# Top-32 attention with a routed expert layer: where three small steps of a row tile's end are put

## The chip, the cores and the metric

One Trainium2 chip, one core. The metric is the device time of one execution in microseconds; it is given as the median of several runs. TensorE (PE), VectorE (DVE), ScalarE (ACT), GpSimd (POOL) and SyncE (SP) each work through a queue of their own in order; semaphores hold an instruction back until others have finished.

## The reference

Attention over 8 batches, 8 heads, 576 rows of 64 features: only the 32 largest scores of a row are kept. Its result is the input of an expert layer: a gate with 8 experts, of which each keeps its 80 best tokens.

```python
scores = scale * np.matmul(q, k.transpose(0, 1, 3, 2))
kth = np.partition(scores, -top_k, axis=-1)[..., -top_k:-top_k + 1]
scores = np.where(scores >= kth, scores, -1000000000.0)
scores = scores - np.max(scores, axis=-1, keepdims=True)
attn = np.exp(scores)
attn = attn / (np.sum(attn, axis=-1, keepdims=True) + 1e-09)
x = np.matmul(attn, v)              # then (B,S,H*D) -> (4608, 512)
...
logits = x @ w_gate
expert_idx = np.argmax(logits, axis=1)
probs = np.exp(logits - logits.max(-1, keepdims=True))
probs /= probs.sum(-1, keepdims=True) + 1e-09
gate_w = probs[np.arange(N), expert_idx]
for e in range(E):                  # at most 80 tokens of each expert
    h = np.maximum(x[tok_idx] @ w1[e], 0.0)
    out[tok_idx] = gate_w[tok_idx, None] * (h @ w2[e])
```

## The kernel before

The attention is done in 32 pairs n (batch, two heads). A pair has five row tiles t: t = 0 to 3 of 128 rows for both heads, and the tail t = 4, which holds the last 64 rows of both heads together. A tile of one head is a unit; a pair has 4 x 2 + 1 = 9 units, 288 in all.

`run` writes the order of all engines by hand. Step i does one unit's worth of every stage, each stage for a unit some steps back. In a step the stages of VectorE's search come in the order of a string of letters, one for even and one for odd i. As a pair has nine steps, a given t falls into odd steps in one pair and into even steps in the next.

The stages, by lines of the kernel before:

- `front` (L229, L236): TensorE's scores of a tile go to a set of four banks of PSUM that `four` hands out (one buffer, `sp`); ScalarE copies them to `s` in SBUF, which frees the banks.
- `parts` and `search` (L244 to L271): VectorE finds 24 large candidates; the last of them (`w`, L255) goes as bias to ScalarE's sign (L260), GpSimd multiplies it with `s` (L266, `y`), VectorE takes the maxima of `y` (L268) and picks the threshold (L271, `pick`).
- `below` (L280 on ScalarE for odd units, L282 on GpSimd for even ones): the mask of the scores under the threshold.
- `turn_w` (L318 to L327), six steps behind: TensorE transposes the scores and adds the masks' products, into `ab` (the first 512 keys) and into one of two banks `cc` (the last 128 keys); ScalarE's exponentials L325 (of `cc`) and L327 (of `ab`) give `wT`.
- `back` (L338): the product of `wT` with v, into other columns of the same `cc`. For the tail, `back` of t = 3 is issued in the same step ahead of the tail's `turn_w`.
- `over` (letter z, L350): VectorE's reciprocals of the sums, one step after `back`.
- `divide` (letter x, L359 or L367): the features are multiplied by the reciprocals, which frees `cc`.
- `norm`, once per pair, some steps later, one part in each step: the pair's features go to DRAM and are transposed (into `sp`), copied to `xT` (L384), multiplied with the gate's weights (L389, 20 small matmuls, into `sp`) and copied (L396, `part`); VectorE adds the parts (L400), and after the eighth head computes the gates.

`turn` (L204, L217) transposes the next pair's q and k, through `sp` as well. After the attention come the routing and the experts' products, which the change doesn't touch. A second path (`batch`), which runs only if a check of the data asks for it, is not executed.

Of the kernel before, what the change touches and what calls it, by code (L numbers as in the profile page):

```python
# [15 lines left out]
Alu = mybir.AluOpType  # L16
# [11 lines left out]
def kernel(  # L28
# [11 lines left out]
    nc = tc.nc  # L40
    B, H, S, D = q.shape
    N, Dm = out.shape
    E = moe_w_gate.shape[1]
# [6 lines left out]
    P = 128  # L50
    HP = H // 2
    NP = B * HP
    NF = S // P
    TL = S - NF * P
    NK = NF + 1
# [43 lines left out]
    minus = const.tile([P, P], BF16, name="minus")  # L99
    nc.scalar.mul(minus, ident, -1.0)  # L100

    huge = const.tile([P, P], BF16, name="huge")
# [46 lines left out]
    class Attention:  # L149
# [152 lines left out]
        def turn_w(self, n, t):  # L302

            i = n * UPP + 2 * t
            g = 2 if t < NF else 1
            if i == NU - 1 and not self.lean:

                ab = self.four().rearrange("p h (c r) -> p h c r", r=P)
            else:
                ab = self.ps_w.tile([P, 2, NF, P], F32, name="ab", tag="ab")  # L310
            cc = self.ps_c.tile([P, 512], F32, name="cc", tag="cc")
            keys = [slice(c * P, c * P + P) for c in range(NF)] + [slice(S - P, S)]
            dst = [[ab[:, h, c, :] for c in range(NF)] + [cc[:, h * P : (h + 1) * P]] for h in range(g)]

            for h in range(g):
                sc = self.s.pop(i + h)
                for c in range(NK):
                    nc.tensor.matmul(dst[h][c], lhsT=sc[:, keys[c]], rhs=ident, start=c == 0 or (c == NF and h == 0), stop=False,  # L318
                                     is_transpose=True, skip_group_check=True)
            for h in range(g):  # L320
                mk = self.mask.pop(i + h)
                for c in (NF, *range(NF)):
                    nc.tensor.matmul(dst[h][c], lhsT=mk[:, keys[c]], rhs=huge if i + h in self.odd else minus, start=False, stop=True, skip_group_check=True)  # L323
            wT = self.rows.tile([P, 2 * NK, P], F32, name="wT", tag="wT")
            nc.scalar.activation(wT[:, 2 * NF : 2 * NF + g, :].rearrange("p h r -> p (h r)"), cc[:, : g * P], Act.Exp,  # L325
                                 scale=scale / TINY)
            nc.scalar.activation(wT[:, : g * NF, :], ab.rearrange("p h c r -> p (h c) r")[:, : g * NF, :], Act.Exp, scale=scale / TINY)  # L327
            self.w[n, t] = wT, cc

        def back(self, n, t):  # L330

            wT, cc = self.w.pop((n, t))
            vb = self.vb[n % len(self.vb)]
            for h in range(2 if t < NF else 1):
                o = slice(2 * P + h * (D + 1), 2 * P + (h + 1) * (D + 1))
                for c in range(NK):
                    for r in range(0, P, TL):
                        nc.tensor.matmul(cc[r : r + TL, o], lhsT=wT[:, h * NF + c if c < NF else 2 * NF + h, r : r + TL],  # L338
                                         rhs=vb[:, c, h if t < NF else r // TL, :], start=(c == 0), stop=(c == NF))
            self.w[n, t] = cc  # L340

        def over(self, n, t):

# [8 lines left out]
        def divide(self, n, t):  # L352
            if t == 0:
                self.xn[n] = self.rows.tile([P, NK, 2, D], F32, name="xn", tag="xn")
            cc = self.w.pop((n, t))
            if t < 2:

                sums = cc[:, 2 * P : 2 * P + 2 * (D + 1)].rearrange("p (h d) -> p h d", h=2)[:, :, :D]
                nc.vector.tensor_tensor(out=self.xn[n][:, t, :, :], in0=sums, op=Alu.mult,  # L359
                                        in1=self.z[:, n % NP, t, :].unsqueeze(2).to_broadcast([P, 2, D]))  # L360
                return
            for h in range(2):
                if t < NF:
                    p, o, j, m = slice(0, P), 2 * P + h * (D + 1), h, P
                else:
                    p, o, j, m = slice(TL * h, TL * h + TL), 2 * P, 0, TL
                nc.scalar.activation(self.xn[n][:m, t, h, :], cc[p, o : o + D], Act.Copy, scale=self.z[p, n % NP, t, j : j + 1])  # L367

        def norm(self, n, b, hp, bi, nb, cs=range(NK)):


            xn = self.xn[n].rearrange("p c h d -> p c (h d)")
            one, cols = bass.ds(b, 1), slice(hp * P, (hp + 1) * P)
            full = [c for c in cs if c < NF]
            if full:
                nc.sync.dma_start(xv[one, : NF * P, cols].rearrange("o (c p) d -> p (o c) d", p=P), xn[:, :NF, :])
            if NF in cs:
                nc.sync.dma_start(xv[one, NF * P :, cols].rearrange("o p d -> p o d"), xn[:TL, NF:, :])
            yield 1
            ps = self.four()[:, :2, :].rearrange("p j c -> p (j c)")  # L380
            at = slice(cs[0] * P, min(S, cs[-1] * P + P))
            self.turn_in(ps, xn, cs)
            xT = self.xT
            nc.scalar.copy(xT[:, at], ps[:, at])  # L384
            yield 1
            lp = self.four()[:, 0, : NK * E].rearrange("p (c e) -> p c e", e=E)
            for c in cs:
                for r in range(0, P, TL):
                    nc.tensor.matmul(lp[r : r + TL, c, :], lhsT=xT[:, c * P + r : c * P + r + TL], rhs=wg[:, hp, :],  # L389
                                     start=True, stop=True)  # L390
            if bi == 0 and hp == 0:
                self.lg = self.small.tile([P, nb, NK, E], F32, name="lg", tag="lg", bufs=2)
            cs = slice(cs[0], cs[-1] + 1)
            lg = self.lg[:, bi, cs]
            part = lg if hp == 0 else self.small.tile([P, NK, E], F32, name="part", tag="part", bufs=2)[:, cs]
            nc.scalar.copy(part, lp[:, cs])  # L396
            yield 0
            yield 0
            if hp > 0:
                nc.vector.tensor_tensor(out=lg, in0=lg, in1=part, op=Alu.add)  # L400
            if hp == HP - 1 and bi == nb - 1 and cs.stop == NK:
                yield 0
                yield from self.gates(b - bi, nb)
# [32 lines left out]
        def run(self, slow):  # L436
# [11 lines left out]
            drawn = []  # L448
            ready = {}

            def whole(i):

                return 0 <= i < NU and units[i][2] > 0

            def step(i, last):
                if 0 <= i < NU:
                    n, t, h = units[i]
# [9 lines left out]


                back = dict(a=0, b=1, c=1, d=1, e=1, y=3, g=4, h=5, m=5, H=4, M=4)
                for c in "GybGcGdGeGGzaxg" if i % 2 else "GGbghHmMyGcGdGeGzax":  # L470
                    if c == "G":
                        if 0 <= i < NU:
                            next(first[i])
                    elif c == "a":
                        if 0 <= i < NU:
                            next(first[i], None)
                            second[i] = self.search(i)
                            next(second[i])
                    elif c == "z":
                        for u in drawn:  # L480
                            self.over(*u)
                    elif c == "x":
                        for u in drawn:
                            self.divide(*u)
                    elif c in "mM":
                        if 0 <= i - back[c] < NU:
                            self.below(i - back[c])
                    elif i - back[c] in second:
                        next(second[i - back[c]])
                done = list(drawn)  # L490
# [9 lines left out]
                if rest:  # L500
                    back()
                if whole(i - LT):
                    self.turn_w(*units[i - LT][:2])

                ends = [(n, range(NK) if n < NP - 1 else range(NF) if t < NF else range(NF, NK))
                        for n, t in done if t == NF or (n == NP - 1 and t == NF - 1)]
# [2 lines left out]
                busy = 0 <= f < NU and units[f][2] != 1  # L509
                if busy:  # L510
                    self.front(*units[f][:2])
                if not rest:
                    back()
                if due and not busy and i > 0:
                    self.turn(due.pop())
                    busy = True
                for g in list(later):
                    if ready[g] and busy and not last:
                        continue
                    busy = busy or ready[g] == 1  # L520
                    ready[g] = next(g, None)
                    if ready[g] is None:
                        later.remove(g)
# [5 lines left out]
            with tc.manual_schedule():  # L529
# [5 lines left out]
                i = -4  # L535
# [394 lines left out]
```

## Time and profile before

| what | value |
|---|---|
| median of 3 runs | 996.66 us (995.37 to 997.83) |
| profiled execution | 994.35 us, span 992.5 us |
| granted TensorE clock, mean | 0.985 |
| end of the attention in the profile | about 864 us |
| busy in the span | PE 873.2, DVE 824.4, ACT 766.8, POOL 625.1 us |
| multiplications of `divide` on VectorE (L359) | 64, 278 ns each |
| activations of `divide` on ScalarE (L367) | 192, 306 to 309 ns each |
| gates' products (L389) | 640 matmuls, 32 groups of 20 |

The page gives busy times of the engines over the span; a group line gives the count, the busy time, the mean length of one instruction and the idle time of its engine just before. A wait line reads: who waited, for whom, us in total, how often, longest. A timeline row reads: start, length, engine, line, operation, output and input, and in brackets the idle time before it with its releaser.

### The profile page before, as it was taken

The page shows a single profiled execution, that of the slowest core. Times are in us where ns is not written, and L with a number is a line of the kernel's source. Part 1 is how long each engine was busy: PE and PEld are TensorE (multiplying, and loading weights), DVE is VectorE, ACT ScalarE, POOL GpSimd, SP SyncE. Part 2 cuts the span into 40 slices and gives each one's busy share as a digit, 9 for nine tenths or more (in the row PEclk, how much of TensorE's full clock was granted, in tenths as well). Part 3 has the DMA queues.
Part 4 walks back from the last instruction along what each step waited for, and adds up shares of the span by engine and source line. Part 5 has one row for each costly group of instructions (what it writes and reads, how often), then busy time and mean ns, then how long its engine had stood idle before and what let it go on. Part 6 is the DMA issues. An engine that isn't in the chain of part 4 may idle for free.

```text
span 992.5 us, 35681 instructions
## 1 busy us (share of the span) xinstructions
PE 873.2 (88%) x13368; PEld 707.4 (71%) x13368; DVE 824.4 (83%) x4992; ACT 766.8 (77%) x1524; POOL 625.1 (63%) x474
## 2 busy tenths in 40 slices
PE   5989999898989898989898989899898988699896
PEld 3667777676767676777777777777676776578786
DVE  5899999899999999999999999999999989361010
ACT  3889989998989898989998989989898988301110
POOL 3677767776777776776677677767777777201111
PEclk9999999999999999999999999999999999879998
DMA  3454443333333232332222222211122200275910
GB/s 72 121 138 113 125 130 89 85 92 92 92 90 81 83 92 81 87 87 71 49 51 50 50 50 50 50 42 46 38 50 50 50 15 15 78 276 184 370 43 28
DMA packets 167798, 85.77 MB, mean 86 GB/s; under 512 B 117696, under 2 KB 154560, under 8 KB 167616
## 3 DMA queue, kind: packets, MB, share of 16 engines
q1 hardware_dynamic: 166592, 80.78, 29.0%
q0 software_dynamic: 1024, 2.62, 0.9%
q8 instruction: 107, 1.75, 0.7%
q14 instruction: 75, 0.61, 0.2%
HBM read 63.19 MB, written 20.19 MB: 84 GB/s over the span
## 4 chain that ended last, share of the span: by engine, by line
DVE 40%; PE 24%; ACT 20%; issue 9%; POOL 6%; DMA 1%; SPq 0%; POOLq 0%; DVEq 0%; ACTq 0%
DVE w L268 12%; DVE cand L244 11%; PE cc L338 7%; ACT sign L260 6%; DVE cand L263 4%; POOL y L266 4%; ACT wT L327 4%; PE yp L814 4%; ACT mask L280 4%; DVE top L255 3%; PE sp L229 3%; DVE pick L271 3%; ACT xn L367 3%; ACT wT L325 2%; PE ab L318 2%
## 5 line engine op out<-in xcount | busy, mean ns | idle before, releaser
L244 DVE MAX8 cand<-s 128x8 f32<-128x96 f32 x1728 | 400.1, 245 | 8.8 <-ACT s L236 8.8
L282 POOL TENSOR_SCALAR mask<-s,thr_all 128x576 bf16<-128x576 f32 x144 | 248.0, 1722 | 226.8 <-DVE pick L271 115.5
L266 POOL TENSOR_TENSOR y<-s,sign 128x576 f32<-128x576 f32 x288 | 363.2, 1282 | 13.8 <-ACT sign L260 13.8
L338 PEld LDWEIGHTS cc<-vb,wT 128*64 128x64 f32 x5760 | 181.6, 138 | 131.1 <-ACT wT L327 119.6
L338 PE MATMUL cc<-vb,wT 128*64 128x65 f32 x5760 | 203.9, 225 | 60.5 <-ACT wT L327 59.4
L268 DVE MAX8 w<-y 128x8 f32<-128x576 f32 x288 | 217.8, 756 | 13.8 <-POOL y L266 7.4
L260 ACT ACTIVATE sign<-s,w 128x576 bf16<-128x576 f32 x288 | 222.8, 774 | 1.2 <-DVE w L255 0.3
L229 PE MATMUL sp<-both 64*128 64x288 f32 (+1 forms) x1280 | 203.1, 437 | 6.4 <-ACT s L236 4.5
L236 ACT ACTIVATE s<-sp 128x1152 f32<-128x1152 f32 (+1 forms) x161 | 166.5, 1035 | 29.9 <-PE sp L229 29.4
L318 PE MATMUL ab<-ident,s 128*128 128x128 f32 x1148 | 177.5, 282 | 0.0
L327 ACT ACTIVATE wT<-ab 128x1024 f32<-128x1024 f32 (+1 forms) x159 | 148.8, 936 | 0.0
L229 PEld LDWEIGHTS sp<-both 64*128 64x128 f32 (+1 forms) x1280 | 106.0, 180 | 46.6 <-ACT s L236 7.9
L318 PEld LDWEIGHTS ab<-ident,s 128*128 128x128 f32 x1148 | 128.0, 142 | 10.1 <-issue 0.8
L255 DVE MAX8 top<-cand 128x8 f32<-128x48 f32 x576 | 115.4, 200 | 4.7
L280 ACT ACTIVATE mask<-s,thr_all 128x576 bf16<-128x576 f32 x144 | 111.9, 777 | 2.8 <-DVE pick L271 2.4
L263 DVE MATCH_REPLACE8 cand<-top,cand 128x48 f32<-128x48 f32 x576 | 110.6, 192 | 0.0
L323 PEld LDWEIGHTS <-mask 128*128 128x128 bf16 x1440 | 94.4, 98 | 1.9
L318 PE MATMUL cc<-ident,s 128*128 128x128 f32 x288 | 80.5, 279 | 8.4 <-ACT xn L367 8.4
L325 ACT ACTIVATE wT<-cc 128x256 f32<-128x256 f32 (+1 forms) x160 | 56.9, 356 | 26.3 <-PE cc L323 25.2
L217 ACT COPY both<-sp 128x1152 f32<-128x1152 f32 x31 | 34.8, 1124 | 29.7 <-PE sp L204 29.7
L826 POOL DMA_INDIRECT out_dram<-y,idx_s x8 | 7.4, 928 | 78.6 <-DVE y L825 78.6
L260 ACT ACTIVATION_READ_ACCUMULATOR sign<-s,w 128x1 f32 x288 | 56.6, 197 | 0.0
(188 smaller groups left out, 994.8 us busy)
## 6 DMA issues: line engine op xcount, KB each, us to landing
w<-in_moe_w_dram SPq DMA_DIRECT2D x10, 2048.0 KB, 12.0
w<-in_moe_w_dram SPq DMA_DIRECT2D x24, 512.0 KB, 3.9
out_dram<-zero SPq DMA_DIRECT2D x9, 1024.0 KB, 5.6
qn<-in_q_dram SPq DMA_DIRECT2D x64, 128.0 KB, 2.6
kn<-in_k_dram SPq DMA_DIRECT2D x64, 128.0 KB, 2.5
vb<-in_v_dram SPq DMA_DIRECT2D x64, 128.0 KB, 2.5
xd<-xn SPq DMA_DIRECT2D x32, 256.0 KB, 2.6
qn<-in_q_dram SPq DMA_DIRECT2D x32, 32.0 KB, 2.5
```

What stands on the lines that cost most here:

```text
L229: nc.tensor.matmul(o, lhsT=qT[d, t * P : t * P + m], rhs=kT[d, j * HS : (j + 1) * HS], start=True, stop=True)
L236: nc.scalar.activation(s[:, j * HS : (j + w) * HS].rearrange("p (j c) -> p j c", c=HS), ps[:, j : j + w, :HS], Act.Copy, scale=TINY)
L244: nc.vector.max(out=cand[:, j, :], in_=s[:, j * S // NG : (j + 1) * S // NG])
L260: nc.scalar.activation(sign, s, Act.Sign, bias=w9[:, 7:8], scale=-1.0, accum_out=cnt)
L263: nc.vector.match_replace(out=cand, in_to_replace=dst, in_values=cand, imm_value=LOW)
L266: nc.gpsimd.tensor_tensor(out=y, in0=s, in1=sign, op=Alu.mult)
L268: nc.vector.max(out=w9[:, 8:], in_=y)
L280: nc.scalar.activation(self.mask[i], self.s[i], Act.Relu, bias=self.thr[:, i : i + 1], scale=-1.0)
L282: nc.gpsimd.tensor_scalar(self.mask[i], self.s[i], self.thr[:, i : i + 1], None, op0=Alu.is_lt)
L318: nc.tensor.matmul(dst[h][c], lhsT=sc[:, keys[c]], rhs=ident, start=c == 0 or (c == NF and h == 0), stop=False, is_transpose=True, skip_gr ...
L327: nc.scalar.activation(wT[:, : g * NF, :], ab.rearrange("p h c r -> p (h c) r")[:, : g * NF, :], Act.Exp, scale=scale / TINY)
L338: nc.tensor.matmul(cc[r : r + TL, o], lhsT=wT[:, h * NF + c if c < NF else 2 * NF + h, r : r + TL], rhs=vb[:, c, h if t < NF else r // TL, ...
```

## The change

- The masks' products of a tile are issued with the two of the last 128 keys (into `cc`) first, then those into `ab`. Before, each head's five products came together.
- The gates' product of `norm` goes into free columns (400 to 439) of the bank `cc` that the latest `back` has used, and no longer into `sp`. Its part of `norm` runs only in a step that has issued a `back`, and then also if the step has a `front`.
- `divide` does all tiles with ScalarE, two activations each (before, t = 0 and 1 were one multiplication on VectorE), and it is issued after the step's `turn_w`, no longer by the letter x.

```diff
+            for h, c in [(h, NF) for h in range(g)] + [(h, c) for h in range(g) for c in range(NF)]:
+                nc.tensor.matmul(dst[h][c], lhsT=self.mask[i + h][:, keys[c]], rhs=huge if i + h in self.odd else minus,
+                                 start=False, stop=True, skip_group_check=True)
             for h in range(g):
-                mk = self.mask.pop(i + h)
-                for c in (NF, *range(NF)):
-                    nc.tensor.matmul(dst[h][c], lhsT=mk[:, keys[c]], rhs=huge if i + h in self.odd else minus, start=False, stop=True, skip_group_check=True)
+                self.mask.pop(i + h)
...
-            self.w[n, t] = cc
+            self.w[n, t] = self.free = cc
...
-            if t < 2:
-
-                sums = cc[:, 2 * P : 2 * P + 2 * (D + 1)].rearrange("p (h d) -> p h d", h=2)[:, :, :D]
-                nc.vector.tensor_tensor(out=self.xn[n][:, t, :, :], in0=sums, op=Alu.mult,
-                                        in1=self.z[:, n % NP, t, :].unsqueeze(2).to_broadcast([P, 2, D]))
-                return
...
-            yield 1
-            lp = self.four()[:, 0, : NK * E].rearrange("p (c e) -> p c e", e=E)
+            yield 2
+            lp = self.free[:, 400 : 400 + NK * E].rearrange("p (c e) -> p c e", e=E)
...
-                for c in "GybGcGdGeGGzaxg" if i % 2 else "GGbghHmMyGcGdGeGzax":
+                for c in "GybGcGdGeGGzag" if i % 2 else "GGbghHmMyGcGdGeGza":
...
-                    elif c == "x":
-                        for u in drawn:
-                            self.divide(*u)
...
                 if whole(i - LT):
                     self.turn_w(*units[i - LT][:2])
+                for u in done:
+                    self.divide(*u)
...
-                    if ready[g] and busy and not last:
+                    if (ready[g] == 1 and busy or ready[g] == 2 and not drawn) and not last:
```

## The prediction

> **What bounds the kernel now.** I read the page's busy times first, then the windows by stage, the waits, the groups by form, and last the timelines of ScalarE (ACT) and VectorE (DVE) over two neighbouring pairs. Attention fills the first 864 us of the span, and only there does the change act.
>
> ```profile
> PE 873.2 (88%) x13368; PEld 707.4 (71%) x13368; DVE 824.4 (83%) x4992; ACT 766.8 (77%) x1524; POOL 625.1 (63%) x474
> ```
>
> ```profile
> 400.00:500.00 100.00, 90.51 (x1347) 72.53 (x1342) 95.43 (x588) 90.03 (x177) 73.28 (x53) 1.00 0.27 71
> ```
>
> In the window (columns PE, PEld, DVE, ACT, POOL) VectorE looks like the bound. The waits say otherwise:
>
> ```profile
> DVE z_all L350 <- PE cc L338: 36.1, 40, 4.2
> ACT both L217 <- PE sp L204: 29.7, 31, 2.1
> ACT s L236 <- PE sp L229: 29.4, 36, 2.4
> ACT wT L325 <- PE cc L323: 25.2, 35, 2.3
> PE sp L389 <- ACT s L236: 15.3, 29, 0.6
> ACT mask L280 <- DVE pick L271: 2.4, 3, 0.9
> ```
>
> ScalarE waits almost only for TensorE, and hardly ever for VectorE (2.4 us in all). VectorE's idle time is spent at the reciprocal L350, waiting for the product with v. So VectorE is heavily loaded but runs ahead; what sets the pace is the loop of ScalarE and TensorE (scores to SBUF, signs, masks, exponentials, product with v). The pace is very even: a pair's first reciprocal starts at 401.07 us and the one two pairs on at 453.04, 51.97 us per two pairs. Two pairs are the period because a pair has nine steps and the two orders of a step alternate.
>
> ```profile
> L367 ACT ACTIVATE xn<-cc,z_all 128x64 f32<-128x64 f32 x128 | 32.5, 306 | 0.2 <-DVE z_all L350 0.2
> ...
> L325 ACT ACTIVATE wT<-cc 128x256 f32<-128x256 f32 x128 | 48.0, 375 | 3.9 <-PE cc L323 2.8 <-PE ab L323 0.3
> ...
> L359 DVE TENSOR_TENSOR xn<-cc,z_all 128x128 f32<-128x128 f32 x64 | 17.8, 278 | 0.3 <-DVE top L255 0.2
> ```
>
> The place where the change bites is the end of a pair. ScalarE there (pair A, whose t = 3 reciprocal falls into an odd step):
>
> ```profile
> 419.33 1.13 ACT L236 ACTIVATE s<-sp 128x1152 f32<-128x1152 f32 x1 [0.64 <-PE sp L229]
> 420.36 0.77 ACT L260 ACTIVATE sign<-s,w 128x576 bf16<-128x576 f32 x1
> ...
> 421.51 0.20 ACT L396 COPY part<-sp 128x40 f32<-128x40 f32 x1
> 421.58 0.80 ACT L280 ACTIVATE mask<-s,thr_all 128x576 bf16<-128x576 f32 x1
> 422.26 0.78 ACT L260 ACTIVATE sign<-s,w 128x576 bf16<-128x576 f32 x1
> ...
> 423.02 0.63 ACT L367 ACTIVATE xn<-cc,z_all 64x64 f32<-64x64 f32 x2
> 423.68 0.39 ACT L325 ACTIVATE wT<-cc 128x256 f32<-128x256 f32 x1
> ...
> 427.46 0.76 ACT L260 ACTIVATE sign<-s,w 128x576 bf16<-128x576 f32 x1
> ...
> 428.22 0.36 ACT L325 ACTIVATE wT<-cc 128x256 f32<-128x256 f32 x1
> ```
>
> and VectorE over the same work (last row: the next pair, B):
>
> ```profile
> 417.36 0.15 DVE L350 RECIPROCAL z_all<-cc 128x2 f32<-128x2 f32 x1
> ...
> 419.85 0.08 DVE L271 DVE_READ_ACCUMULATOR pick<-past,cnt,w 128x1 f32 x1
> ...
> 420.78 0.19 DVE L255 MAX8 w<-cand 128x8 f32<-128x48 f32 x1
> ...
> 426.67 0.19 DVE L255 MAX8 w<-cand 128x8 f32<-128x48 f32 x1
> ...
> 443.76 0.17 DVE L350 RECIPROCAL z_all<-cc 128x2 f32<-128x2 f32 x1 [0.20 <-PE cc L338]
> ```
>
> The reciprocal of t = 3 runs at 417.36, while ScalarE reaches the end of the step before it (L236 gives way at 420.36) 3.0 us later. In pair B the two are 443.76 and 446.87, 3.1 us apart. This lead is what the change takes away.
>
> **The masks' order.** For the tail tiles (g = 1) the new order equals the old one. For the other 128 the exponential of cc waited 3.9 us in all, so an earlier cc saves at most that; and the second exponential still needs the last mask product. Worth 0.
>
> **The divisions.** VectorE loses 64 multiplications of 278 ns, at most 17.8 us; it is not the bound, so 0 on the path. ScalarE gains 128 activations. A single one lasts 306 ns, but two in a row hold the engine 0.39 us (413.94 to the next start at 414.33), so 64 x 0.39 = 25 us, 1.56 us per two pairs (195 ns each, which the sum uses). All divisions now stand behind the exponentials of their step, so those for t = 2 and the tail (0.65 us) no longer delay the exponentials, and what follows overlaps the product with v. Part is absorbed in ScalarE's waits: t = 0's 0.39 falls ahead of L217, which waits 0.62 and 1.23 us (absorbed); t = 1's falls ahead of the copy of xT, which waits 0.49 in B (0.1 left) and nothing in A (0.39 left); for t = 2 the exponentials gain 0.39 where TensorE waits for them. Net: B's second half gains 0.29, A's 0.
>
> The Trainium skill ("ScalarE: Activation LUTs", Rules for kernel authors) says to put multiplications on VectorE, not ScalarE, which speaks against this part. By that page's costs (What ACT_TABLE_LOAD costs: 186 ns, 93 for a pointer operand, 0.833 an element, 93 overlapped) an estimate is 240 ns each, 30.7 us in all, or 1.92 us per two pairs.
>
> **The gates' product.** Its 20 matmuls (0.76 us) no longer wait for L236 to free the score banks (15.3 us in 29 cases), and move ahead of the tail's product with v; the copy of the logits moves one step earlier, directly behind L236. TensorE is not what ScalarE waits for next at this place, so the gain is 0. But the product now lies in the bank that holds t = 3's sums, and in the program as built the reciprocal of t = 3 waits on ScalarE's count after the copy of the logits, no longer on the product with v alone. VectorE's whole queue stands behind it.
>
> The Trainium skill ("PSUM — Partial Sum Buffer", PSUM bank collisions raise a hardware error) tells to guard a bank and not an address, since two engines on disjoint columns of one bank collide. No row of this trace shows a collision; by it the wait can't be dropped.
>
> Pair A, counting from L, the moment L236 gives way (420.36 before). Copy 0.2, and about 0.1 to VectorE (my estimate, from the 0.05 to 0.1 between a releaser and its follower in these rows): reciprocal at L + 0.3. From VectorE's rows: the threshold that the mask needs is there 419.93 - 417.36 = 2.57 later, the w that the next sign needs 3.61, the w of two steps on 9.50 later. ScalarE: sign, two divisions, then the mask must wait until L + 2.9 (before: 421.58, L + 1.2); the sign until L + 3.96; exponentials L + 4.72 (before 423.68, L + 3.32); the tail's division 0.65, L236 1.03, sign 0.76; a second mask; the next sign waits for its w until L + 9.85, and the next exponentials start at L + 10.61. Before: 428.22, L + 7.86. Loss 2.75; 0.15 comes back, since the addition of the logits (0.58 us) now fills a gap before a wait for y. With B's gain of 0.29: 2.75 - 0.15 - 0.29 = 2.3 us.
>
> Pair B: the mask stands before the reciprocal in the order and doesn't wait; the next w comes 1.5 us behind it, in time. The exponentials wait for TensorE, whose transposes wait for t = 3's divisions (448.91 against 448.80), so they start as before; the tail's division, once ahead of them, now follows: about 0.5 us.
>
> Per two pairs 2.8 us. With 16 A pairs and 15 B pairs that have a pair behind them, 16 x 2.3 + 15 x 0.5 = 44.3 us. On the profiled execution (span 992.5, time 994.35) that is 1038.7; the median before is 2.3 us higher, 1041. I take 1040.
>
> Ends for the unknown parts: if only the first mask and sign are late, A loses 1.4 - 0.29 = 1.1 and B nothing: 16 x 1.1 = 18, 1012 to 1014. If nothing is absorbed (B's gain fails, t = 1's 0.39 counts in both), A loses 3.1 and B 1.0: 65 us, 1059 to 1062. I am nearer to the middle, since the VectorE rows between reciprocal and w are full of work whose order does not change.
>
> **Rivals.** (1) The wait is taken from VectorE's lead and costs ScalarE nothing. For it: VectorE idles 4.6 us in 100 and sheds 17.8. Against: the mask has only 421.58 - 419.93 = 1.65 us of slack, and the lead lost is 3.3. Then only the divisions count, B's 0.5 less 0.2 per two pairs: 16 x 0.3 = 5 us, 1000.
>
> (2) Faster. The exponentials are off the divisions, and TensorE's waits for wT (59.4 us) shrink; if every division is absorbed where ScalarE waits for TensorE (4.9 us per two pairs), 0.39 + 0.65 per two pairs come off: 16 x 1.04 = 17 us, 980. It decides if VectorE reaches t = 3's reciprocal no earlier than ScalarE finishes the copy; before, it was 3 us ahead.
>
> (3) The stall spreads: TensorE waits for both, A and B each lose the whole 3.3 us: 31 x 3.3 = 102, 1095 at most; I expect half of it, 1070.
>
> (4) The masks' order doing nothing is already in the forecast.
>
> **How the numbers follow.** Forecast 0.79 (own range 1012 to 1062), rival 1 0.09, rival 2 0.05, rival 3 0.07. The range 1014 to 1060 leaves out rival 1, rival 2, most of rival 3 and the last edges of the forecast. About 0.3%, 3 us, is what a measurement of this kernel can tell from no change; rival 1 lies on that edge and gives 0.04 to "same": faster 0.05, same 0.04, slower 0.91.
>
> **What would show it.** Right: the reciprocal of t = 3 has some 3 us of idle time in front of it in every pair, released by the copy of the logits; mask L280 and sign L260 show waits for pick and w in every other pair, 1.5 us or more; the period of two pairs is 54.8 us; VectorE's busy share of a window falls to about 89%; the waits of the exponential of cc are no smaller. Wrong: if the reciprocal is released by the product with v, or if ScalarE never waits for VectorE, the forecast fails and rival 1 or 2 holds; if ScalarE's busy time in a window rises above 93, the pace has not fallen.

## The result, and the profile after

The changed kernel takes 1028.67 us (median; 1024.72 to 1029.41) against 996.07 us of the kernel before: ratio 1.0317, 95% interval 1.0287 to 1.0347. Its profiled execution has a span of 1026.9 us, 34.4 us more than before.

The page's busy times and one window of the attention (columns PE, PEld, DVE, ACT, POOL):

```profile
PE 876.4 (85%) x13368; PEld 707.7 (69%) x13368; DVE 807.5 (79%) x4928; ACT 796.7 (78%) x1652; POOL 624.8 (61%) x474
```

```profile
400.00:500.00 100.00, 87.36 (x1284) 69.31 (x1279) 87.57 (x551) 89.62 (x186) 68.72 (x49) 1.00 0.29 76
```

Over the span VectorE lost 16.9 us of work and ScalarE got 29.9 us more, but every engine's share of the window fell: all of them wait. Who for, the waits tell:

```profile
DVE z_all L352 <- ACT part L392: 57.5, 22, 2.9
...
ACT both L217 <- PE sp L204: 21.2, 31, 2.1
...
ACT wT L327 <- PE cc L322: 19.5, 34, 1.9
DVE z_all L352 <- ACT lg L392: 19.1, 8, 3.1
ACT mask L280 <- DVE pick L271: 18.2, 19, 1.1
...
DVE z_all L352 <- PE cc L340: 9.9, 4, 4.1
ACT sign L260 <- DVE w L255: 8.9, 29, 0.6
```

and, before, for the last of them:

```profile
ACT sign L260 <- DVE w L255: 0.3, 1, 0.3
```

L352 and L392 are the reciprocal and the copy of the logits (L350 and L396 before). The reciprocal waits 76.6 us for the copy (the rows `part` and `lg` together), in 30 of 32 pairs, where it never waited for it before. ScalarE's two waits for VectorE, 18.2 us for pick and 8.9 us for w (2.4 and 0.3 before), together 27.1 us, are most of the 34.4 us that the loop pays.

The end of a pair A on ScalarE's timeline, and on VectorE's:

```profile
434.46 1.13 ACT L236 ACTIVATE s<-sp 128x1152 f32<-128x1152 f32 x1 [0.64 <-PE sp L229]
435.49 0.19 ACT L392 COPY part<-cc 128x40 f32<-128x40 f32 x1
...
437.97 0.78 ACT L280 ACTIVATE mask<-s,thr_all 128x576 bf16<-128x576 f32 x1 [1.12 <-DVE pick L271]
439.07 0.78 ACT L260 ACTIVATE sign<-s,w 128x576 bf16<-128x576 f32 x1 [0.32 <-DVE w L255]
...
444.59 0.78 ACT L260 ACTIVATE sign<-s,w 128x576 bf16<-128x576 f32 x1 [0.24 <-DVE w L255]
...
445.37 0.36 ACT L327 ACTIVATE wT<-cc 128x256 f32<-128x256 f32 x1
```

```profile
435.71 0.17 DVE L352 RECIPROCAL z_all<-cc 128x2 f32<-128x2 f32 x1 [2.67 <-ACT part L392]
...
439.30 0.18 DVE L396 TENSOR_TENSOR lg<-lg,part 128x40 f32<-128x40 f32 x1
...
444.31 0.19 DVE L255 MAX8 w<-cand 128x8 f32<-128x48 f32 x1
...
464.05 0.17 DVE L352 RECIPROCAL z_all<-cc 128x2 f32<-128x2 f32 x1 [2.85 <-ACT part L392]
...
490.06 0.17 DVE L352 RECIPROCAL z_all<-cc 128x2 f32<-128x2 f32 x1 [2.54 <-ACT part L392]
```

The last two rows are t = 3's reciprocals of pair B and of the next pair A.

L, where L236 gives way, is 435.49. The reciprocal starts 0.22 us behind it after 2.67 us of idling; the mask, the sign and the sign two steps on each wait for what VectorE finds after it; the second exponentials start at L + 9.88, before at L + 7.86. From one tail's reciprocal to the one two pairs on it is now 54.36 us (384.69 to 439.05) against 51.96 (421.05 to 473.01).

### The profile page after: what moved, and what is told of

It is laid out like the page before. It is cut to its first block, busy times and chain, and to the rows that moved or that the text cites. A ratio compares the mean times of both kernels' runs of the same rounds, so it can differ in the third digit from the quotient of the medians.

```text
span 1026.9 us, 35737 instructions
## 1 busy us (share of the span) xinstructions
PE 876.4 (85%) x13368; PEld 707.7 (69%) x13368; DVE 807.5 (79%) x4928; ACT 796.7 (78%) x1652; POOL 624.8 (61%) x474
## 5 line engine op out<-in xcount | busy, mean ns | idle before, releaser
L260 ACT ACTIVATE sign<-s,w 128x576 bf16<-128x576 f32 x288 | 225.8, 784 | 10.3 <-DVE w L255 8.9
L236 ACT ACTIVATE s<-sp 128x1152 f32<-128x1152 f32 (+1 forms) x161 | 167.9, 1043 | 30.3 <-PE sp L229 29.6
L318 PE MATMUL ab<-ident,s 128*128 128x128 f32 x1148 | 177.8, 282 | 0.0
L318 PEld LDWEIGHTS ab<-ident,s 128*128 128x128 f32 x1148 | 128.0, 142 | 11.5 <-issue 0.8
L280 ACT ACTIVATE mask<-s,thr_all 128x576 bf16<-128x576 f32 x144 | 113.4, 788 | 18.6 <-DVE pick L271 18.2
L318 PE MATMUL cc<-ident,s 128*128 128x128 f32 x288 | 80.8, 281 | 29.3 <-ACT xn L363 29.3
L352 DVE RECIPROCAL z_all<-cc 128x2 f32<-128x2 f32 (+1 forms) x160 | 24.8, 155 | 86.5 <-ACT part L392 57.5
L363 ACT ACTIVATE xn<-cc,z_all 128x64 f32<-128x64 f32 (+1 forms) x320 | 86.5, 319 | 1.2 <-DVE z_all L352 0.8
L327 ACT ACTIVATE wT<-cc 128x256 f32<-128x256 f32 (+1 forms) x160 | 56.5, 353 | 19.5 <-PE cc L322 19.5
L318 PEld LDWEIGHTS cc<-ident,s 128*128 128x128 f32 x288 | 40.7, 141 | 36.7 <-ACT xn L363 36.7
```

The source lines that it names most:

```text
L236: nc.scalar.activation(s[:, j * HS : (j + w) * HS].rearrange("p (j c) -> p j c", c=HS), ps[:, j : j + w, :HS], Act.Copy, scale=TINY)
L260: nc.scalar.activation(sign, s, Act.Sign, bias=w9[:, 7:8], scale=-1.0, accum_out=cnt)
L280: nc.scalar.activation(self.mask[i], self.s[i], Act.Relu, bias=self.thr[:, i : i + 1], scale=-1.0)
```

## The experiments

Three theories were kept apart: the wait (the reciprocal behind the copy takes VectorE's lead), the divisions (ScalarE sets the pace and got more work), and the bank itself (TensorE and ScalarE at work in a bank of the sums).

| kernel | masks' order | divisions behind exponentials | t = 0, 1 on ScalarE | gates' product | ratio (95%) |
|---|---|---|---|---|---|
| before | old | no | no | score banks | 1 |
| after | new | yes | yes | sums' bank, ahead of the reciprocal | 1.0317 (1.0287 to 1.0347) |
| e1 | old | no | no | as after | 1.0429 (1.0398 to 1.0459) |
| e2 | new | yes | yes | score banks | 0.9999 (0.9987 to 1.0011) |
| e3 | old | yes | no | score banks | 0.9937 (0.9925 to 0.9949) |
| e4 | old | no | yes | score banks | 1.0256 (1.0239 to 1.0273) |
| e5 | new | no | no | score banks | 1.0000 (0.9979 to 1.0020) |
| e6 | new | behind L236 too | yes | sums' bank, behind the reciprocal | 1.0112 (1.0090 to 1.0134) |
| e7 | old | behind L236 too | no | as e6 | 1.0141 (1.0118 to 1.0163) |
| e8 | new | yes | no | score banks | 0.9904 (0.9883 to 0.9925) |
| e9 | new | yes, t = 3 behind the copy | yes | t = 3's bank, behind its reciprocal | 1.0016 (0.9999 to 1.0033) |
| e10 | new | as e9 | no | as e9 | 0.9931 (0.9912 to 0.9950) |
| e11 | old | no | no | score banks; the wait alone added | 1.0449 (1.0423 to 1.0476) |

**e1, the bank alone.** Before, with these lines of the change:

```diff
-            self.w[n, t] = cc
+            self.w[n, t] = self.free = cc
...
-            yield 1
-            lp = self.four()[:, 0, : NK * E].rearrange("p (c e) -> p c e", e=E)
+            yield 2
+            lp = self.free[:, 400 : 400 + NK * E].rearrange("p (c e) -> p c e", e=E)
...
-                    if ready[g] and busy and not last:
+                    if (ready[g] == 1 and busy or ready[g] == 2 and not drawn) and not last:
```

> Before with the gates' product in the bank of t = 3's sums alone; masks' order and divisions as before. The theory of the wait (the reciprocal of t = 3 stands behind ScalarE's copy of the logits, and takes VectorE's lead of 3 us): nearly the whole loss, about 2.2 us per two pairs, 16 x 2.2 = 35 us, ratio 1.03 to 1.04, and a wait of 2.5 to 3 us before L350 for the copy in every pair. The theory of the divisions (ScalarE sets the pace and got 25 us more work): no loss, ratio 1.00.

Measured: 1.0429, more than the whole change, with 83.5 us of waits of L350 for the copy (29 times). The theory of the divisions falls as the cause of the loss. The size was 43 us against the 35 expected. ScalarE's waits for pick and w are 19.4 and 10.3 us, hardly more than in the changed kernel (18.2 and 8.9), so they don't explain the excess; where it lies stays open.

**e2, all but the bank.** The changed kernel with those lines turned back.

> The changed kernel with the gates' product back in the score banks; masks' order and divisions as changed. The wait: VectorE keeps its lead, the rest costs about 0.3 us per two pairs, 5 us, ratio 1.005. The divisions: most of the loss stays, ratio 1.02 to 1.03.

Measured: 0.9999. Without the product in the bank the whole change is worth nothing, and the product in its bank costs 1028.67 - 995.22 = 33 us. Against the expected 5 us it came out even; in the profile the two-pair period, 52.22 us (422.70 to 474.92), is 0.26 above that of before, as the expected 0.3, and the last reciprocal of the attention comes 3.1 us later (862.46 against 859.41).

**e3, the place of the divisions alone.**

```diff
-                for c in "GybGcGdGeGGzaxg" if i % 2 else "GGbghHmMyGcGdGeGzax":
+                for c in "GybGcGdGeGGzag" if i % 2 else "GGbghHmMyGcGdGeGza":
...
-                    elif c == "x":
-                        for u in drawn:
-                            self.divide(*u)
...
                 if whole(i - LT):
                     self.turn_w(*units[i - LT][:2])
+                for u in done:
+                    self.divide(*u)
```

> Before with the divisions only moved behind the exponentials of their step; t = 0 and 1 still on VectorE. By the prediction's steps the exponentials after t = 2 start 0.39 us earlier (gain 0.3 to 0.4 in each pair), and the tail's 0.65 us come to stand in ScalarE's way in pair B (loss 0.55): 0 within 5 us, ratio 0.995 to 1.005. If TensorE's wait for wT were what sets the pace, all of 0.39 + 0.65 us per pair would come off: ratio 0.97 to 0.98.

Measured: 0.9937, a gain of 6 us, just outside what was expected. In the profiles the last reciprocal of the attention comes 3.2 us earlier (856.18 against 859.41), and what follows that reciprocal is 3.6 us shorter, though the change doesn't touch the routing and the experts' products there. This second part is not explained: over the profiles of this study (one of each kernel) that last stretch takes 127.6 to 132.0 us in the eight kernels with the divisions behind the exponentials and 133.1 to 135.1 us in the five others.

**e4, ScalarE's extra divisions alone**, at the old place: the branch `if t < 2` is never taken.

> Before with t = 0 and 1 divided by ScalarE too, at the old place ahead of the exponentials. If ScalarE's and TensorE's loop sets the pace, 4 x 0.39 us per two pairs are in it unhidden: 16 x 1.56 = 25 us, ratio 1.015 to 1.025. If VectorE sets the pace, its 64 multiplications come off: 13 to 18 us less, ratio 0.982 to 0.987.

Measured: 1.0256, 24 us, what 64 x 0.39 = 25 us gives if nothing is hidden. VectorE, with the highest busy share in the window of the attention, got 64 instructions less, and the kernel lost what ScalarE was given: VectorE did not set the pace. The Trainium skill ("Perfetto Trace Analysis", Identifying the Most-Contended Engine) says to optimize the engine with the highest occupancy first. Of the engines that the page judges by occupancy, that is VectorE in this window (95%); this run speaks against the rule for this kernel, though it relieves VectorE and loads ScalarE at once. VectorE now waits longer for the product with v:

```profile
DVE z_all L350 <- PE cc L338: 66.0, 70, 4.2
```

against 36.1 us before.

**e5, the masks' order alone.**

> Before with the masks' order changed alone. The wait: nothing, 996 within 2 us, since the exponential of cc waited 3.9 us in all for the tiles whose order changes. If the exponentials' start were what sets the pace: up to 128 x 0.3 us earlier, 960 to 990.

Measured: 1.0000. **e8, the masks' order on top of e3:**

> The kernel with the divisions only moved behind the exponentials (0.994 of before), with the masks' order changed too. Now ScalarE comes to the exponential of cc 0.4 to 0.65 us earlier after t = 2 and the tail, and may find it not ready: a gain of up to 0.3 us in one or two tiles of a pair, ratio 0.985 to 0.994; 0.994 if the second exponential, which needs all masks, ends the wait anyway.

Measured: 0.9904, against 0.9937 of e3, each against its own runs of the kernel before; the intervals touch (0.9925), so the order's own share is not settled. In the profiles the last reciprocal of the attention comes only 1.6 us earlier than in e3 (854.62 against 856.18). The exponential of cc waits 16.2 us in all, 20.6 in e3. This is the fastest kernel of the study, 984.24 us.

**e6 and e7, the product behind the reciprocal.** (The edit is shown against the changed kernel, for e6.) The bank is that of a tile whose reciprocal is already issued; so that TensorE need not wait for ScalarE's divisions of that tile, all divisions were put at the end of the step.

```diff
-                for u in done:
-                    self.divide(*u)
...
+                if done:
+                    self.free = self.w[done[-1]]
...
-                    if (ready[g] == 1 and busy or ready[g] == 2 and not drawn) and not last:
+                    if (ready[g] == 1 and busy or ready[g] == 2 and not done) and not last:
...
+                for u in done:
+                    self.divide(*u)
```

> The changed kernel, with the gates' product still in a bank of the sums, but issued behind the reciprocal of that bank's tile (and the divisions behind the copy): nothing of VectorE waits for the copy any more. The theory of the wait: the loss is gone, VectorE's lead of 3 us is back, ratio 0.99 to 1.00 like the kernel with the product in the score banks (1.000). If the bank itself costs (TensorE and ScalarE at work in the same bank, or the copy's earlier place in ScalarE's order): 1.02 to 1.03.

> A candidate better than both: t = 0 and 1 divided on VectorE, all divisions behind the exponentials, the gates' product in a bank of the sums behind its reciprocal. The wait: TensorE's 0.5 us for L236 per pair goes, VectorE keeps its lead: ratio 0.985 to 0.995 against 0.994 without the bank. If the bank costs: 1.01 to 1.03.

Measured: 1.0112, between both theories, and 1.0141, inside what was expected of e7 if the bank costs. The reciprocal no longer waits for the copy in either (in e7 the multiplications L359 do, 6.6 us in all). Both have a long wait of TensorE (e6):

```profile
PE cc L318 <- ACT xn L363: 43.0, 30, 1.7
```

Before, this wait (of L318 for L367) was 8.4 us; in the changed kernel it is 29.3. The divisions had moved behind the front's L236 as well, and `turn_w` needs the bank that they free. In the profiles the product also lies in t = 2's bank, not in t = 3's: e6 copies the logits at 426.31 us, ahead of t = 3's reciprocal at 427.59. So these two runs mix several causes and tell nothing sure on the bank.

**e9, the same without that delay.** Only t = 3's divisions stand behind the copy; the product goes into t = 3's bank, one step later than in the changed kernel (the step in which it was issued before the change), where there is no front.

```diff
+                sums = [u for u in done if u[1] == NF - 1]
                 for u in done:
-                    self.divide(*u)
+                    if u not in sums:
+                        self.divide(*u)
...
+                if sums:
+                    self.free = self.w[sums[-1]]
...
-                    if (ready[g] == 1 and busy or ready[g] == 2 and not drawn) and not last:
+                    if (ready[g] == 1 and busy or ready[g] == 2 and not sums) and not last:
...
+                for u in sums:
+                    self.divide(*u)
```

> The changed kernel with the gates' product in the bank of t = 3's sums, but issued one step later, behind that tile's reciprocal and the tail's product with v; only t = 3's divisions stand behind the copy, all others at once behind the exponentials. In the run before this one, all divisions stood behind the front's copy L236, and TensorE's transposes into cc waited 43 us for them (30 waits), so that run had two causes mixed. If the bank itself is free and that delay was the cost: 0.99 to 1.00, like the kernel with the product in the score banks (1.000). If the bank costs: 1.01 again.

Measured: 1.0016. The bank costs next to nothing once the reciprocal does not stand behind the copy (0.9999 with the product in the score banks). No wait of the reciprocal for the copy is left, but one of TensorE is:

```profile
PE cc L318 <- ACT xn L363: 30.3, 30, 1.3
```

That is 12.7 us less than in e6, and 21.9 more than with the product in the score banks (8.4 in e2): TensorE's transposes into the bank wait for t = 3's divisions, which stand behind the copy. As e9 differs from e6 in the bank and the step of the product too, how much of e6's loss came from the delayed divisions is not shown. **e10** does the same to e8:

> The best kernel so far (t = 0 and 1 on VectorE, divisions behind the exponentials, masks of the last keys first: 0.990), with the gates' product placed in the same way, behind t = 3's reciprocal. The wait: 0.985 to 0.992, TensorE's 0.5 us per pair for L236 being gone but not what ScalarE waits for. If the bank costs: 1.00 or more.

Measured: 0.9931, just outside what was expected and no better than e8. TensorE's wait of L389 for L236 (15.3 us in e8) is gone, but its wait of L318 for the divisions has grown from 8.4 us in e8 to 30.2. So the run shows that this placing brings nothing; what it would be worth to free TensorE from L236 alone is not shown.

**e11, the wait alone.**

```diff
+                if rest:
+                    seen = self.small.tile([P, 1], F32, name="seen", tag="seen", bufs=2)
+                    nc.scalar.copy(seen, self.w[units[i - LT - 1][:2]][:, 2 * P + D : 2 * P + D + 1])
```

> Before, unchanged but for one instruction per pair: ScalarE reads one column of t = 3's sums (128x1, into a small tile that nobody uses) directly behind the L236 of the tail's step, so that the reciprocal of t = 3 has the wait of the changed kernel and nothing is moved. The theory of the wait: nearly what the product in the bank cost alone (1.043), 1.03 to 1.045, with 2.5 to 3 us of idle time before L350 in every pair. If the cost came from the product's new place in TensorE's order, or from the copy's: 1.00 to 1.005.

Measured: 1.0449. One reading of one column per pair costs 44 us, though the 32 readings themselves keep ScalarE busy for only 4.9 us in all. Its waits:

```profile
DVE z_all L350 <- ACT seen L514: 86.0, 32, 5.8
...
ACT mask L280 <- DVE pick L271: 19.5, 25, 1.1
...
ACT sign L260 <- DVE w L255: 10.3, 33, 0.3
```

The same three waits as in the changed kernel, though neither a product, nor a division, nor a mask was moved. That the wait is the cause is shown by e2 and e9 (without it) and by e11 (with nothing else). e11 is the one that decides: e2 and e9 also put the product back into the step it had before.

## Why the prediction was right, step by step

The direction, the mechanism and the place held: the reciprocal of t = 3 idles in front of the copy (2.5 to 2.9 us in most of the rows between 380 and 550 us, 1.6 in one; some 3 forecast), ScalarE then waits for pick and w in every other pair, VectorE's share of a window fell to 88 (89 forecast), and the period of two pairs is 54.36 us (54.8). One sign was too large: the waits for pick and w were to be 1.5 us or more, and are 1.12 and 0.32 us in most of those pairs. The change cost 34.4 us in the profiles against 44.3 forecast, inside the range but below its point.

The first term below rests on GpSimd's two multiplications y and VectorE's second maximum of y, here before and then after:

```profile
416.47 2.53 POOL L266 TENSOR_TENSOR y<-s,sign 128x576 f32<-128x576 f32 x2
...
419.03 0.76 DVE L268 MAX8 w<-y 128x8 f32<-128x576 f32 x1
```

```profile
432.07 2.52 POOL L266 TENSOR_TENSOR y<-s,sign 128x576 f32<-128x576 f32 x2
...
437.05 0.75 DVE L268 MAX8 w<-y 128x8 f32<-128x576 f32 x1
```

By terms:

- **Pair A's loss, 2.3 us forecast.** From the reciprocal of pair A to that of B it is now 464.05 - 435.71 = 28.34 us, where L to L was 26.51: 1.83. The step that was mis-sized is the stretch from the reciprocal to the w two steps on, 9.50 us in the rows of before. Here it is 444.50 - 435.71 = 8.79, and the two shorter ones are 2.23 (forecast 2.57) and 3.26 (3.61). The rows of before were taken while VectorE ran ahead, close behind GpSimd. Before, GpSimd's two y ended at 419.00 and the second maximum began at 419.03. After the stall y lay ready (its row ended at 434.59, before the reciprocal), and the same instructions went through 0.35 us faster. The addition of the logits, 0.58 us in the rows of before, was 0.18 at its new place, which is most of the rest. So the second mask did not wait at all, and the exponentials came at L + 9.88, not L + 10.61: 2.02 us late, not 2.75. Of the 0.44 us that the sum then took back (0.15 and 0.29), only 2.02 - 1.83 = 0.19 was seen, which hid a part of that error.
- **Pair B's loss, 0.5 us forecast:** 490.06 - 464.05 = 26.01 against 25.46 (446.87 to 472.33 before), 0.55. Right.
- **Per two pairs** 2.38 us, 2.8 forecast; 16 x 1.83 + 15 x 0.55 = 37.5 us, of which the last reciprocal of the attention shows 35.5 (894.87 against 859.41).
- **The wait alone** costs more (43 and 44 us in e1 and e11) than on top of the other changes (33 us, the changed kernel against e2). The sum has no term for that, and no run takes it apart.
- **The divisions.** That their 25 us would largely be absorbed behind the exponentials held: ahead of them they cost 24 us (e4), behind them 0.9999 - 0.9904 of 995, some 9 us (e2 against e8, each against its own runs of before; by the last reciprocals of the two profiles, 7.8 us). A part of it is seen at L217, which waits 30.3 us in e8 and 21.7 in e2. That the move by itself is worth nothing failed a little: it gained 6 us (e3).
- **The masks' order at 0** holds alone (e5).
- **The gates' product off L236 at 0** is neither shown nor refuted: in e9 and e10 another wait of TensorE, for the divisions, grew by 22 us.
- **"The waits of the exponential of cc are no smaller"** was wrong: 25.2 us before, 19.5 after. Moving the divisions behind the exponentials alone already lowers them, to 20.6 (e3).

The rivals: that the wait costs ScalarE nothing, and that all divisions are absorbed for a gain, both fall with the two waits of ScalarE for VectorE. The third, that the stall spreads to both pairs, did not come: B lost 0.55 us. Its price was miscounted: half of 102 us on 994 is some 1045, not 1070, which lies inside the stated range, so only the profile could tell it from the forecast.

## What to carry to other kernels

An engine with the highest busy share may still be running ahead, as VectorE did here; its lead is what lets the pacing engines find their inputs ready. Before a small product is put into the unused columns of a bank, look at who reads the bank's other columns and on whom they would have to wait: here a copy of 0.2 us, standing behind ScalarE's copy of the scores (L236), held back VectorE's whole queue for 2.7 us. The order can be chosen: the same product behind the reciprocal cost next to nothing, and the same divisions cost 24 us ahead of the exponentials and about 9 behind them.

## What the runs showed of the hardware

VectorE's addition of two 128x40 tiles in SBUF (the logits) took 0.58 to 0.67 us in 21 of the 23 rows of the kernel before and 0.18 us in the other two and in all 23 rows after, with the same shapes. In the slow rows it began while GpSimd was in the multiplication y or about 0.12 us into a mask; in the quick ones GpSimd was idle, or its mask's row had begun about 1.04 us earlier.

The Trainium skill ("SBUF — State Buffer", Who interferes with whom) says that a VectorE instruction with two inputs in SBUF contends with a GpSimd instruction that reads SBUF. The rows agree with it except that some quick ones lie inside a mask's row, whose ends are rough on GpSimd; no run here takes the two apart.
